# Two attention and two spectral layers on one core: unit sums rounded a round's end later, a quad's first loads spread out, output weights split earlier

## The chip, the core and the metric

The kernel runs on one core of a Trainium2 chip. The time is device microseconds (us) of one execution, and lower is better. The core's engines work side by side and wait for one another by semaphores: TensorE (PE; its weight loads are shown apart as PEld), VectorE (DVE), ScalarE (ACT), GpSimd (POOL) and SyncE (SP), which here only issues DMAs. Each engine runs its own instructions in the order in which the program emits them, so moving a line of the program moves an instruction in one or more of these queues.

## The reference, cut to what matters

```python
def _A_ref(x, wqkv, wo):                 # B, S, D = 1, 2048, 576; H, Dh, W = 32, 18, 256
    q, k, v = split_heads(x @ wqkv)
    scores = einsum("bhqd,bhkd->bhqk", q, k) * (Dh ** -0.5)
    mask = (idx[:, None] - idx[None, :] >= 0) & (idx[:, None] - idx[None, :] < W)
    p = softmax(where(mask, scores, -1e9))
    return merge_heads(einsum("bhqk,bhkd->bhqd", p, v)) @ wo

def _B_ref(x, w_r, w_i):
    return irfft2(rfft2(x) * (w_r + 1j * w_i))

x = x + _A_ref(_layernorm(x), A_wqkv, A_wo)
x = x + _B_ref(_layernorm(x), B_w_r, B_w_i)
x = x + _A_ref(_layernorm(x), A_wqkv, A_wo)
x = x + _B_ref(_layernorm(x), B_w_r, B_w_i)
```

All in float32. The kernel keeps that precision on PE by writing an operand as a rounded part (the "high" part, type fp32r in the profile) plus the remainder.

## The kernel before

Each attention layer (the change is in both, which are called layer 1 and layer 2 here) takes the 32 heads as eight **quads** n of four heads, and each quad as 16 blocks of 128 tokens. That gives 128 **value blocks** t in a row. A block of queries needs the keys of its own block and of the two before it. For every block and head there are two scores: S, by which the maximum of a row is found (`score_max`: PE L1187, then DVE L1189), ten blocks ahead (`LEAD`), and E, the score with the maximum already subtracted (`exps`: PE L1219), of which ACT takes the exponential (L1220). POOL then cuts the exponentials to the window by two selects (L1222, L1225), and PE multiplies them by the values (`part`, U, L1240); DVE turns the result (L1246).

`mixed()` runs the first 118 blocks in 59 **rounds** p = 0 to 58 of two blocks each (t = 2p and 2p + 1); the other ten blocks are the **tail**. A round has sixteen items, eight of `score_max` and eight of `exps`, and between them PE works on the projection of the queries and keys that later quads need (matmuls L1115 into `pj` and `pk`). After the items come U of the two blocks before and its turning. S, E, `pj` and `pk` live in banks of PSUM, of which E has three and S three.

The projection is cut into **units**, 128 rows of queries or keys by 512 tokens. 23 of them close within the rounds, at p = 1, 3, 5, 7, 9, 11, 13, 15, 18, 20 and so on to 48 (`ends`, two rounds apart at first, two or three from 13 on). When a unit closes in round e, ACT copies its two halves from PSUM to a staging tile `sg` (L1129; two buffers, used in turn). Four steps follow:

- `total`: POOL adds the halves, at the end of round e, as its last items.
- `high`: ACT rounds the sum (L1136).
- `remainder`: POOL subtracts the rounded part from the sum (L1142).
- `send`: SP stores both parts to `qk_d` in DRAM (L1145, 512 KB).

Where the steps stand is written out by hand with three lists for each round: `early` runs after the round's first item, `mid` after the eighth (the middle, between the exponentials of the two blocks), and `end` after the sixteenth, before U. After the eighth item, and after U, the round also calls `behind(t)`, which issues the output projection's preparations.

`loads(t)` brings queries and keys of a quad back from `qk_d` (`stack_load`, L1162), 512 tokens at a time in four **pieces** of three DMAs of 72 KB: pieces 0 and 1 are queries (`qs`), 2 and 3 keys (`ks`). Each of `qs` and `ks` has two buffers, one for the even quads and one for the odd ones. Quad 1 comes in by t = 4 to 15, one piece a block. Quad 2's first 512 tokens come at t = 12 to 15, beside quad 1's last 512 tokens. From there on each quad has one piece a block. SP issues DMAs in order, and each has to wait its turn behind the DMAs ahead of it on that queue.

The attended result goes through DRAM (`op_d`, `o_d`) to the output projection (`Out`). Its tiles (`room`) take the place of the projection's input; its weights come in five DMAs (`weights`, L744), each a fifth. `split(k)` rounds a fifth on ACT (L751) and takes the remainder (L752): on POOL for k = 0 to 2, on DVE for k = 3 and 4. `OB` is 120. The weights are loaded at t = 104 to 112 and split at t = 110 to 118, so the last split stands at the start of the tail. After the tail the attended result is read back (`oraw`) and multiplied by the weights (`ops`, L802).

Of the kernel before, what the change touches and what calls it, by code (L numbers as in the profile page):

```python
# [8 lines left out]
F32 = mybir.dt.float32  # L9
# [706 lines left out]
class Out:  # L716
# [32 lines left out]
    def split(self, k):  # L749
        c = slice(2 * self.n * k, 2 * self.n * (k + 1))  # L750
        self.nc.scalar.copy(self.w["h"][:, c], self.raw[:, c])  # L751
        (self.nc.vector if k > 2 else self.nc.gpsimd).tensor_sub(self.w["l"][:, c], self.raw[:, c], self.w["h"][:, c].bitcast(F32))  # L752

    def const(self, k):

# [110 lines left out]
def layer_a(tc, ident, eps, bp, big, src, dst, wqk_d, wv_d, wo_d, dc_d, gc_d, dram, copy, wvs, second, spectral, share):  # L866
# [17 lines left out]
    if True:  # L884
# [191 lines left out]
        with ExitStack() as c2:  # L1076
# [224 lines left out]
            def loads(t):  # L1301
                if t + LEAD in (0, 2):
                    stack_load(0, 2 + (t + LEAD) // 2)
                if t == -4:
                    stack_load(1, 0)
                n, c = divmod(t + (12 if t < 16 else 20), NT)
                if 4 <= t < 16 or 1 < n < NQ and t >= 12:
                    stack_load(1 if t < 16 else n, t // 4 if t < 16 else c // 4, (t % 4,))
                if 12 <= t < 16:
                    stack_load(2, 0, (t % 4,))  # L1310
                if t + LEAD == 5:
                    v_load(0)
                if t + 12 in range(NT, NX, NT):
                    v_load((t + 12) // NT)
# [24 lines left out]
            def mixed():  # L1339
# [4 lines left out]
                early, mid, end = {}, {}, {}  # L1344
                plan = lambda d, p, f, *a: d.setdefault(p, []).append((f, a))
# [5 lines left out]
                for p in range(last):  # L1351
# [33 lines left out]
                    done += n  # L1385
                    for total, high, remainder, send in ended:
                        total()
                        for f in (high, remainder):
                            plan(mid, p + 1, f)
                        plan(mid, p + 2, send)  # L1390
                    ended.clear()
                    run(end, p)
                    if p:
# [6 lines left out]
                    else:  # L1400
                        if p:
                            n, c = divmod((2 * p - 1) // 4, 4)
# [15 lines left out]
            OB = NX - 8  # L1418
            out = Out(nc, eps, bp, big, o_d, srcv, dstv, wo_d, dc_d, gc_d, second)

            def behind(t):
                if copy and t >= 32 and t % 4 == 0 and t < 32 + 16 * len(copy):

                    z, r = divmod(t // 4 - 8, 4)
                    P.dma_start(*[a[32 * r:32 * r + 32] for a in copy[z]])
                if t == OB - 16:
                    out.room()
                if t - OB + 16 in range(0, 10, 2):
                    out.weights((t - OB + 16) // 2)
                if 0 <= t - (OB - 10) < 10 and t % 2 == 0:  # L1430
                    out.split((t - (OB - 10)) // 2)
                if t - OB + 13 in range(0, 10, 2):
                    out.const((t - OB + 13) // 2)
                if t == OB - 3:
                    out.filters()
                if t - OB + 8 in range(0, 10, 2):
                    out.load_x(((t - OB + 8) // 2 + 1) % 5)
                if 0 <= t - (OB - 8) < 6:
                    out.attended(*divmod(t - (OB - 8), 2))
                if t - OB in (1, 2):  # L1440
                    out.attended(3, t - OB - 1)
                if t == OB + 4:
                    out.ahead_of_last()
                if t - OB - 5 in (0, 1, 2):
                    out.turn(t - OB - 5, V)
                if t == NX:

                    A.activation(wp.tile([128, 1], F32, name="se", bufs=1), eps, AF.Sqrt)
# [90 lines left out]
```

## Time and profile before

| | before |
|---|---|
| time, median of 3 runs | 1326.73 us (1315.5, 1326.73, 1673.2) |
| the profiled execution's own time | 1323.85 us |
| its span in the trace | 1322.1 us |
| mean granted clock of PE in it | 0.994 |
| rounds of layer 1, layer 2 (in the trace, from 128.8 and 805.7 us) | 59 each, mostly 4.9 to 5.5 us |

The profile gives the busy time of each engine, the waits (which instruction's idle time was ended by which other one), groups of instructions by line, and stretches of time with each engine's busy time. In a row of the time-ordered view the first number is the start, the second the duration in us, then the engine, the line and the tiles (out<-in); "x4" folds four instructions, and a bracket says how long the engine had stood idle before and what ended that. A row of the stretches has start:end, then length, and for PE, PEld, DVE, ACT and POOL the busy time with the number of instructions; the last three numbers are the granted clock (1.00 is full speed), the DMA engines' mean busy share, and GB/s.

### The profile page before, as it was taken

What the parts mean: (1) busy time and instruction counts of PE and PEld (TensorE: products, weight loads), DVE (VectorE), ACT (ScalarE), POOL (GpSimd) and SP (SyncE); (2) the same over time, 40 slices, a digit from 0 to 9 for tenths busy, and PEclk for the clock granted to TensorE, in tenths of its full rate; (3) what the DMA queues carried; (4) which work ended last, traced back from release to release, by engine and by line L of the source; (5) the groups of instructions that cost most, each with busy time, mean ns of one, the idle gap of its engine ahead of it and who ended that gap; (6) DMA issues with size and microseconds to landing.
All of it is one profiled execution on the core that took longest, in us unless ns stands there. A gap on an engine that the chain in (4) does not pass through costs nothing.

```text
span 1322.1 us, 35482 instructions
## 1 busy us (share of the span) xinstructions
PE 1281.5 (97%) x12115; PEld 1005.3 (76%) x12115; DVE 956.0 (72%) x3196; ACT 777.0 (59%) x1944; POOL 771.0 (58%) x1248
## 2 busy tenths in 40 slices
PE   8999999999999899999999999999999999899998
PEld 8986666666678699975999976666666686897687
DVE  5417889889899577757674148888889896676755
ACT  5522777878777545533355315777877778473233
POOL 2258777898776443567221196788878767113811
PEclk9999999999999999999999999999999999999999
DMA  6846666665566646688873368576665667498874
GB/s 202 220 153 206 209 199 219 213 213 193 192 199 218 199 120 225 198 261 258 275 264 74 89 204 224 194 212 195 199 199 184 201 207 247 137 346 266 287 237 164
DMA packets 179497, 274.37 MB, mean 208 GB/s; under 512 B 67743, under 2 KB 77727, under 8 KB 177989
## 3 DMA queue, kind: packets, MB, share of 16 engines
q1 hardware_dynamic: 167007, 243.63, 58.7%
q0 software_dynamic: 4656, 13.44, 3.8%
q10 hardware_dynamic: 7654, 15.03, 3.2%
q8 instruction: 97, 1.59, 0.5%
q14 instruction: 83, 0.68, 0.2%
HBM read 164.54 MB, written 114.81 MB: 211 GB/s over the span
## 4 chain that ended last, share of the span: by engine, by line
PE 80%; ACT 6%; DMA 5%; DVE 4%; issue 2%; SPq 1%; POOL 1%; DVEq 0%; ACTq 0%; POOLq 0%
PE U L1240 11%; PE pj L1115 10%; PE vps L1005 9%; PE S L1187 8%; PE ops L802 7%; PE pk L1115 6%; PE E L1219 6%; PE po L274 4%; ACT P L1220 4%; PE pq L524 3%; PE p L503 2%; PE pf L274 2%; PE pi L600 2%; PE pz L312 1%; DMA ks<-qk_d 1%
## 5 line engine op out<-in xcount | busy, mean ns | idle before, releaser
L1189 DVE CUSTOM_DVE_ANT_0 jk<-S,mask 128x384 bf16<-128x384 f32 (+2 forms) x1024 | 482.8, 527 | 35.1 <-PE S L1187 13.3
L1220 ACT ACTIVATE P<-E 128x384 f32<-128x384 f32 (+2 forms) x1024 | 409.3, 487 | 95.4 <-PE E L1219 49.7
L1219 PE MATMUL E<-qs,ks 64*128 64x384 f32 (+2 forms) x1024 | 324.3, 372 | 7.2 <-ACT P L1220 4.5
L1187 PE MATMUL S<-ks,qs 63*128 63x384 f32 (+2 forms) x1024 | 325.0, 370 | 5.6 <-DMA qs<-qk_d 2.7
L1222 POOL TENSOR_SCALAR_AFFINE_SELECT P<-P 128x512 f32<-128x512 f32 x256 | 162.3, 634 | 133.5 <-ACT P L1220 125.3
L1219 PEld LDWEIGHTS E<-qs,ks 64*128 64x128 f32 x1024 | 180.6, 185 | 63.1 <-ACT P L1220 42.1
L1187 PEld LDWEIGHTS S<-ks,qs 63*128 63x128 f32 x1024 | 172.7, 185 | 66.0 <-DVE m L1189 37.8
L1240 PE MATMUL U<-P,vq 128*32 128x256 f32 (+2 forms) x3840 | 185.1, 329 | 0.0
L1240 PEld LDWEIGHTS U<-P,vq 128*32 128x32 f32 (+1 forms) x3840 | 107.1, 109 | 75.4 <-POOL P L1225 16.3
L1115 PE MATMUL pj<-xh,wqh 64*128 64x512 f32 (+1 forms) x360 | 154.9, 430 | 0.0
L1225 POOL TENSOR_SCALAR_AFFINE_SELECT P<-P 128x512 f32<-128x512 f32 x224 | 144.0, 643 | 0.0
L1115 PE MATMUL pj<-xh,wql 64*128 64x512 f32 (+1 forms) x360 | 138.6, 425 | 0.0
L1115 PE MATMUL pj<-xl,wqh 64*128 64x512 f32 (+1 forms) x288 | 120.4, 418 | 0.0
L802 PE MATMUL ops<-oroom 128*128 128x290 f32 (+1 forms) x812 | 114.0, 297 | 1.7 <-DVE ofree L848 1.2
L802 PEld LDWEIGHTS ops<-oroom 128*128 128x128 f32 x812 | 110.4, 189 | 2.3 <-ACT ofree L836 1.5
L1115 PE MATMUL pk<-xh,wqh 64*128 64x512 f32 x230 | 92.2, 401 | 0.0
L1115 PE MATMUL pk<-xh,wql 64*128 64x512 f32 x230 | 91.1, 400 | 0.0
L1246 DVE STREAM_TRANSPOSE us<-U 128x256 f32<-128x256 f32 x128 | 57.1, 446 | 46.6 <-PE U L1240 45.6
L1189 DVE DVE_READ_ACCUMULATOR2_ANT m<- 128x1 f32 x1024 | 84.9, 83 | 0.0
L1115 PE MATMUL pk<-xl,wqh 64*128 64x512 f32 x184 | 73.1, 397 | 0.0
L1115 PEld LDWEIGHTS pj<-xh,wqh 64*128 64x128 f32 (+1 forms) x360 | 66.8, 186 | 7.5 <-issue 1.5
L789 POOL TENSOR_TENSOR oroom<-oraw,oroom 64x128 fp32r<-64x128 f32 x26 | 13.9, 535 | 99.1 <-ACT oroom L787 49.2
(522 smaller groups left out, 2869.6 us busy)
## 6 DMA issues: line engine op xcount, KB each, us to landing
qk_d<-sg SPq DMA_DIRECT2D x56, 512.0 KB
qs<-qk_d SPq DMA_DIRECT2D x384, 72.0 KB
ks<-qk_d SPq DMA_DIRECT2D x348, 72.0 KB
op_d<-o SPq DMA_DIRECT2D x56, 256.0 KB
v_d<-vt SPq DMA_DIRECT2D x32, 304.0 KB
vq<-v_d SPq DMA_DIRECT2D x16, 608.0 KB
wt<-in_w SPq DMA_DIRECT2D x16, 580.0 KB
ofree<-x SPq DMA_DIRECT2D x16, 580.0 KB
```

The costliest lines, as they stand in the source:

```text
L274: T.matmul(ps[:, c, 0:NF], tail[r] if si == 4 else hl_(si), dcs[b // 2][r, b % 2], start=mi == si == 0, stop=si == 4)
L802: self.nc.tensor.matmul(self.ps[u][n][:, 0:self.n], x, self.w[p][:, (2 * wk + n) * self.n:(2 * wk + n + 1) * self.n], start=first and i == ...
L1005: T.matmul(ps[:, n, 0:288], xT(xk, c), w[:, wk, n * 288:(n + 1) * 288], start=i == 0, stop=i == len(ks) - 1)
L1115: T.matmul(ps.rearrange("r (n p) -> r n p", n=NT) if second else ps, w[r, wk], x[r], start=s == 0, stop=s == len(ks) - 1)
L1187: T.matmul(ps[:, 0:N], q[b:b + 63, pair, i * 128:i * 128 + 128], k[b:b + 63, pair, lo:hi], start=True, stop=True)
L1189: V.tensor_tensor_reduce(out=jk[:, 0:N], in0=ps[:, 0:N], in1=mask[:, 384 - N:384], scale=1.0, scalar=-3e38, op0=ALU.add, op1=ALU.max, accu ...
L1219: T.matmul(ps[:, 0:nq], k[b:b + 64, pair, j * 128:j * 128 + 128], q[b:b + 64, pair, j * 128:j * 128 + nq], start=True, stop=True)
L1220: A.activation(p[:, hl_, 0:nq], ps[:, 0:nq], AF.Exp, scale=SC)
L1222: P.affine_select(out=p[:, :, 0:128], in_=p[:, :, 0:128], pattern=[[0, 4], [1, 128]], compare_op=ALU.is_ge, fill=0.0, base=0, channel_mult ...
L1225: P.affine_select(out=p[:, :, 256:384], in_=p[:, :, 256:384], pattern=[[0, 4], [-1, 128]], compare_op=ALU.is_gt, fill=0.0, base=0, channel ...
L1240: T.matmul(U[32 * h:32 * h + v.shape[1], (q0 - e) * 128:(q1 - e) * 128], v, pt[n, j][:, h, (q0 - j) * 128:(q1 - j) * 128], start=j == max( ...
L1246: V.transpose(us[n, c][:, 8 * k:8 * k + 8].rearrange("r b (a p) -> r (b a) p", a=2), U[:, 0:256].rearrange("r (p n) -> r n p", n=NT))
```

## The change

Four places change. The rounding `high` goes from the middle of round e + 1 to its end, `remainder` from there to the early list of round e + 2, and `send` from the middle of round e + 2 to its end. Quad 2's first four pieces are loaded at t = 6, 8, 10 and 12 instead of 12 to 15. The output's `room` and weights come at t = 98 to 106 instead of 104 to 112 and are split at t = 104 to 112 instead of 110 to 118 (the rounds in the title of the change count value blocks t). The remainders of all five fifths are taken by POOL.

```diff
--- before.py
+++ after.py
@@ -749,7 +749,7 @@
     def split(self, k):
         c = slice(2 * self.n * k, 2 * self.n * (k + 1))
         self.nc.scalar.copy(self.w["h"][:, c], self.raw[:, c])
-        (self.nc.vector if k > 2 else self.nc.gpsimd).tensor_sub(self.w["l"][:, c], self.raw[:, c], self.w["h"][:, c].bitcast(F32))
+        self.nc.gpsimd.tensor_sub(self.w["l"][:, c], self.raw[:, c], self.w["h"][:, c].bitcast(F32))
 
     def const(self, k):
 
@@ -1306,8 +1306,8 @@
                 n, c = divmod(t + (12 if t < 16 else 20), NT)
                 if 4 <= t < 16 or 1 < n < NQ and t >= 12:
                     stack_load(1 if t < 16 else n, t // 4 if t < 16 else c // 4, (t % 4,))
-                if 12 <= t < 16:
-                    stack_load(2, 0, (t % 4,))
+                if t in range(6, 14, 2):
+                    stack_load(2, 0, ((t - 6) // 2,))
                 if t + LEAD == 5:
                     v_load(0)
                 if t + 12 in range(NT, NX, NT):
@@ -1385,9 +1385,9 @@
                     done += n
                     for total, high, remainder, send in ended:
                         total()
-                        for f in (high, remainder):
-                            plan(mid, p + 1, f)
-                        plan(mid, p + 2, send)
+                        plan(end, p + 1, high)
+                        plan(early, p + 2, remainder)
+                        plan(end, p + 2, send)
                     ended.clear()
                     run(end, p)
                     if p:
@@ -1423,12 +1423,12 @@
 
                     z, r = divmod(t // 4 - 8, 4)
                     P.dma_start(*[a[32 * r:32 * r + 32] for a in copy[z]])
-                if t == OB - 16:
+                if t == OB - 22:
                     out.room()
+                if t - OB + 22 in range(0, 10, 2):
+                    out.weights((t - OB + 22) // 2)
                 if t - OB + 16 in range(0, 10, 2):
-                    out.weights((t - OB + 16) // 2)
-                if 0 <= t - (OB - 10) < 10 and t % 2 == 0:
-                    out.split((t - (OB - 10)) // 2)
+                    out.split((t - OB + 16) // 2)
                 if t - OB + 13 in range(0, 10, 2):
                     out.const((t - OB + 13) // 2)
                 if t == OB - 3:
```

On ACT, layer 1, round 6 (the unit `sg_3` closed in round 5; `P_12` and `P_13` are the exponentials of the round's two blocks). Before:

```order
L1220 ACTIVATE P_12_3124<-E_0_3125 128x384
L1220 ACTIVATE P_12_3124<-E_1_3136 128x384
L1220 ACTIVATE P_12_3124<-E_2_3139 128x384
L1220 ACTIVATE P_12_3124<-E_3_3148 128x384
L1136 CAST sg_3_3081<-sg_3_3081 128x512
L1220 ACTIVATE P_13_3170<-E_0_3171 128x384
L1220 ACTIVATE P_13_3170<-E_1_3180 128x384
L1220 ACTIVATE P_13_3170<-E_2_3183 128x384
L1220 ACTIVATE P_13_3170<-E_3_3192 128x384
```

and with the change, the same place:

```order
L1220 ACTIVATE P_12_3124<-E_0_3125 128x384
L1220 ACTIVATE P_12_3124<-E_1_3136 128x384
L1220 ACTIVATE P_12_3124<-E_2_3139 128x384
L1220 ACTIVATE P_12_3124<-E_3_3148 128x384
L1220 ACTIVATE P_13_3168<-E_0_3169 128x384
L1220 ACTIVATE P_13_3168<-E_1_3178 128x384
L1220 ACTIVATE P_13_3168<-E_2_3181 128x384
L1220 ACTIVATE P_13_3168<-E_3_3190 128x384
L1136 CAST sg_3_3080<-sg_3_3080 128x512
```

The rounding moved from between the two blocks' exponentials to behind the last one. The same holds at 46 places, 23 in each layer.

On SP, layer 1, about rounds 5 to 7 (`qs_1058` and `ks_1060` are the buffers of quads 0 and 2, `qs_1059` and `ks_1061` those of quad 1; L1203 writes the maxima of a row beside the queries). Before:

```order
L1203 DMA qs_1059<-mt_0_2213 2x4x128 x2
L1162 DMA qs_1059<-qk_d 18x2x512 x3
L1162 DMA qs_1058<-qk_d 18x2x512 x3
L1162 DMA qs_1059<-qk_d 18x2x512 x3
L1162 DMA qs_1058<-qk_d 18x2x512 x3
L1162 DMA ks_1061<-qk_d 18x2x512 x3
L1162 DMA ks_1060<-qk_d 18x2x512 x3
L1275 DMA op_d<-o_1_2309 128x512
L1145 DMA qk_d<-sg_3_2182 128x2x512
L1162 DMA ks_1061<-qk_d 18x2x512 x3
L1162 DMA ks_1060<-qk_d 18x2x512 x3
L1203 DMA qs_1059<-mt_1_2445 2x4x128 x2
```

and with the change:

```order
L1203 DMA qs_1059<-mt_0_2222 2x4x128 x2
L1162 DMA qs_1059<-qk_d 18x2x512 x3
L1162 DMA ks_1060<-qk_d 18x2x512 x3
L1162 DMA qs_1059<-qk_d 18x2x512 x3
L1162 DMA ks_1061<-qk_d 18x2x512 x3
L1275 DMA op_d<-o_1_2313 128x512
L1162 DMA ks_1061<-qk_d 18x2x512 x3
L1145 DMA qk_d<-sg_3_2190 128x2x512
L1203 DMA qs_1059<-mt_1_2445 2x4x128 x2
```

Of quad 2's four pieces only the last one (`ks_1060`) still stands among quad 1's last four, and the send of `sg_3` stands behind quad 1's last piece instead of ahead of it. The other three pieces have moved to rounds 3, 4 and 5.

On DVE, layer 1, the last round (58). Before:

```order
L1189 ISA jk_1_0_7964,m_3_7823<-S_1_0_7962,mask 128x384
L1189 ISA m_3_7823 128x1
L752 TENSOR_TENSOR oroom<-ofree,oroom 128x576
L1189 ISA jk_0_1_7972,m_3_7823<-S_0_1_7970,mask 128x384
L1189 ISA m_3_7823 128x1
```

and with the change:

```order
L1189 ISA jk_1_0_7968,m_3_7829<-S_1_0_7966,mask 128x384
L1189 ISA m_3_7829 128x1
L1189 ISA jk_0_1_7974,m_3_7829<-S_0_1_7972,mask 128x384
L1189 ISA m_3_7829 128x1
L1189 ISA jk_1_1_7984,m_3_7829<-S_1_1_7982,mask 128x384
```

The subtraction of the output weights no longer stands between the maxima; it is on POOL, six blocks sooner.

## The prediction

> **What bounds the kernel now.** I read the page's shares first, then who waits for whom, then the value rounds one by one. TensorE (PE) looks like the bound:
>
> ```profile
> PE 1281.5 (97%) x12115; PEld 1005.3 (76%) x12115; DVE 956.0 (72%) x3196; ACT 777.0 (59%) x1944; POOL 771.0 (58%) x1248
> ```
>
> But a busy PE is modelled, and the waits name a partner:
>
> ```profile
> PEld E L1219 <- ACT P L1220: 42.1, 137, 1.3
> POOL P L1222 <- ACT P L1220: 125.3, 155, 3.8
> ```
>
> 137 times PE's weight load for the second score (E) stands until ACT has emptied a bank by an exponential; GpSimd (POOL) mostly waits for ACT too, so it keeps up. The rounds say when. Here are six pairs of rounds from layer 1, by their stretches (start:end, length, then busy time of PE, PEld, DVE, ACT, POOL). The two of a pair have the same place in a quad (p mod 8): p = 24 and 40, 26 and 42, 13 and 29, 22 and 38, 39 and 23, 41 and 25. In the second of each, the rounding of a unit (high, L1136) stands between the exponentials.
>
> ```profile
> 255.38:260.29 4.91, 4.91 (x65) 3.39 (x64) 4.81 (x18) 4.52 (x11) 3.21 (x7) 1.00 0.60 185
> 336.68:341.84 5.16, 5.16 (x63) 3.37 (x62) 4.95 (x18) 3.98 (x10) 4.76 (x7) 1.00 0.38 119
> 265.01:269.92 4.91, 4.91 (x63) 3.41 (x62) 4.81 (x18) 4.53 (x11) 4.31 (x8) 1.00 0.58 165
> 346.32:351.71 5.39, 5.32 (x64) 3.50 (x63) 5.10 (x19) 4.32 (x12) 5.39 (x8) 1.00 0.42 121
> 199.13:204.26 5.13, 5.13 (x68) 3.39 (x65) 4.50 (x19) 4.35 (x10) 3.48 (x7) 1.00 0.78 250
> 280.55:286.04 5.49, 5.39 (x67) 3.36 (x63) 4.58 (x19) 3.82 (x9) 5.48 (x8) 1.00 0.78 229
> 245.17:250.09 4.92, 4.92 (x63) 3.42 (x62) 4.82 (x18) 4.54 (x11) 4.40 (x9) 1.00 0.55 180
> 326.46:331.61 5.15, 5.15 (x65) 3.40 (x64) 4.94 (x18) 3.95 (x10) 5.14 (x8) 1.00 0.36 107
> 331.61:336.68 5.07, 5.07 (x67) 3.59 (x64) 4.49 (x19) 3.23 (x10) 3.34 (x6) 1.00 0.79 275
> 250.09:255.38 5.29, 5.19 (x69) 3.72 (x65) 4.68 (x20) 2.97 (x10) 5.06 (x7) 1.00 0.87 264
> 341.84:346.32 4.48, 4.48 (x51) 2.91 (x47) 4.34 (x19) 3.82 (x10) 2.31 (x5) 1.00 0.75 247
> 260.29:265.01 4.72, 4.72 (x52) 2.88 (x49) 4.64 (x20) 3.81 (x10) 4.18 (x6) 1.00 0.76 250
> ```
>
> PE issues the same work in both of a pair and shows as full in both, yet the second takes 0.25, 0.48, 0.36, 0.23, 0.22 and 0.24 us longer: 0.30 on the mean. So PE is not what sets a round; a loop of PE, DVE and ACT is, and a cast of ACT in its middle stretches it. What comes next is DVE: it is busy 4.81 of 4.91 in the short rounds, so they can't go much lower than these pairs show.
>
> **The cast, moved.** Round 12 shows how, in time order:
>
> ```profile
> 196.00 0.64 ACT L1136 CAST sg<-sg 128x512 fp32r<-128x512 f32 x1
> 196.51 1.67 ACT L1220 ACTIVATE P<-E 128x384 f32<-128x384 f32 x4
> 197.08 0.18 PEld L1219 LDWEIGHTS E<-qs,ks 64*128 64x128 f32 x1 [0.34 <-ACT P L1220]
> ...
> 199.64 1.66 ACT L1220 ACTIVATE P<-E 128x384 f32<-128x384 f32 x4 [1.46 <-PE E L1219]
> ...
> 203.05 0.61 ACT L1129 COPY sg<-pj 128x512 f32<-128x512 f32 x1
> ```
>
> The cast holds up the second block's exponentials, E waits 0.34 us for its bank, and the last score and U behind it on PE start late. After its last exponential ACT then idles 1.46 us while PE does U. There the change puts the 0.64 us cast, so it is hidden; if that cover were gone, it would cost the next round's first exponential 0.64 us at most. In round 13 (199.13 to 204.26, the short one of its pair) the copies of a closing unit stand at that very place (203.05), and cost nothing there. The cast waits for GpSimd's sum, made one round before; behind it wait the exponentials of the next round. The price per rounding is between 0 (all of it given back) and 0.48 (the largest pair); I take the mean, 0.30. There are 23 a layer; those of p = 2 and 8 stand beside a wait for a DMA, so I count 21: 42 × 0.30 = **12.6 us**.
>
> The remainder goes from the middle of round e+1 to the start of e+2 on GpSimd: 1.28 us (L1142, below) leave the round where POOL was busy 4.76 of 5.16 and enter one with 3.21 of 4.91. Behind it wait the selects of that round, which PE reads only in the next round's U: a round of cover, so nothing. The send follows it on SyncE (SP), half a round later; the loads that read it come at least four rounds after the unit closes. Nothing, unless SP jams (last rival).
>
> **The loads, spread.** SP runs ahead of the rounds until a wait stops it. Round 8 ends in a stall in both layers:
>
> ```profile
> 142.86 1.05 SPq L1162 DMA_DIRECT2D ks<-qk_d  x3
> 147.46 0.36 SPq L896 DMA_DIRECT2D wqr<-in_wqk  x1
> ...
> 161.44 4.46 SPq L1162 DMA_DIRECT2D qs<-qk_d  x12
> 165.94 2.95 SPq L1162 DMA_DIRECT2D ks<-qk_d  x6
> ...
> 169.45 1.58 SPq L1145 DMA_DIRECT2D qk_d<-sg  x1
> 171.08 3.00 SPq L1162 DMA_DIRECT2D ks<-qk_d  x6
> ...
> 176.95 0.41 PE L1187 MATMUL S<-ks,qs 63*128 63x384 f32 x1 [1.59 <-DMA qs<-qk_d]
> ...
> 853.28 0.41 PE L1187 MATMUL S<-ks,qs 63*128 63x384 f32 x1 [1.21 <-DMA ks<-qk_d]
> ```
>
> The first S of round 9 needs the last piece of quad 1, issued from 171.08 on, 5.9 us before PE gets it. Ahead of it from 161.44 on stand 18 DMAs, three pieces of quad 1 and three of quad 2 (three DMAs each), and the send of 1.58 us. Now one of them goes into SP's idle stretch from 143.91 to 147.46, two into rounds 4 and 5 (ahead of pieces of quad 1 that round 7 needs; the first of those sits behind a shorter wait, since the send there steps back too), only one stays between quad 1's last pieces, and the send stands behind. That is two pieces fewer after 161 (about 1.05 us each, by the first row) and 1.58: up to 3.7 us sooner, of which the two moved to rounds 4 and 5 may give 2.1 back as a later start. Between 1.6 and 3.7, against a stall of 1.59 and 1.21 and a round 9 that starts about 0.9 us earlier through the casts: I take the stalls as gone, **2.8 us**; at worst they stay.
>
> The first stall also costs clock. These are stretches on the grid of 3.41 us on which the granted clock changes (the third number from the end), then rounds 9 of the two layers:
>
> ```profile
> 175.47:178.88 3.41, 1.68 (x12) 1.32 (x14) 1.55 (x6) 0.82 (x3) 0.55 (x1) 1.00 0.46 138
> 178.88:182.29 3.41, 3.41 (x20) 3.00 (x18) 2.63 (x9) 2.40 (x7) 1.22 (x2) 0.50 0.78 267
> 448.51:451.92 3.41, 1.68 (x34) 0.76 (x32) 2.35 (x5) 1.93 (x4) 0.85 (x2) 1.00 0.91 217
> ...
> 176.95:183.38 6.43, 6.17 (x47) 4.80 (x47) 4.67 (x18) 4.30 (x10) 1.94 (x4) 0.73 0.68 225
> 853.28:858.11 4.83, 4.76 (x49) 3.30 (x49) 4.15 (x18) 3.86 (x10) 1.59 (x3) 1.00 0.54 176
> ```
>
> After a stretch with PE busy 1.68 of 3.41 us the clock was halved for one stretch, and round 9 took 6.43 instead of 4.83: **1.6 us**, which go with the stall. The stretch at 448.51, just as idle, was spared: it stands on the edge. With everything before it shifted on the grid it will more likely be caught, so I set **1.6 us against** it. The Trainium skill ("TensorE: Matmul & The Clock Gate", section "HAM oscillation") has as its abstract rule "no PE-idle gaps >~3.4µs". By that a stall of 1.59 us would halve nothing, and none of the 1.6 would follow from it; the trace agrees with the page on the grid of 3413 ns, not on the length of the gap.
>
> **The output weights.** Per layer five ACT casts and five subtractions; two of these go from DVE to GpSimd.
>
> ```profile
> L752 POOL TENSOR_TENSOR oroom<-ofree,oroom x6: 1407/1414/1428, 414.5 to 1100.8; 128x576 fp32r<-128x576 f32 x3, 128x580 fp32r<-128x580 f32 x3
> ...
> L1142 POOL TENSOR_TENSOR sg<-sg x46: 1266/1282/1297, 142.5 to 1060.8; 128x512 fp32r<-128x512 f32 x46
> ...
> 428.98 0.69 ACT L751 CAST oroom<-ofree 128x576 fp32r<-128x576 f32 x1
> 429.70 0.79 DVE L752 TENSOR_TENSOR oroom<-ofree,oroom 128x576 fp32r<-128x576 f32 x1 [0.32 <-ACT oroom L751]
> ...
> 435.44 0.67 ACT L751 CAST oroom<-ofree 128x576 fp32r<-128x576 f32 x1
> 436.00 12.29 ACT L1220 ACTIVATE P<-E 128x384 f32<-128x384 f32 x34
> ```
>
> Rounds 52, 53 and 54 each get a cast in their middle: +3 × 0.30, by the pairs. Round 57 loses its one: −0.30. In round 58 DVE no longer waits 0.32 and subtracts 0.79 between scores: −1.1. In the tail ACT is without a pause for 12.29 us, so the cast at 435.44 counts in full: −0.56. Sum −1.1 a layer, **2.1 us**; at worst nothing, if the chain of DMAs behind (oraw) keeps its time. The two extra subtractions of 1.41 us lie on GpSimd in rounds that hold no remainder any more. On that queue the selects stand behind them, with a round of cover. The five weight loads on SP (L744) come up to three rounds sooner, just after the last unit has closed (round 48) and its buffers are free; they now stand ahead of the last pieces of quad 7, whose first reader is ten blocks away: nothing.
>
> **Sum.** 12.6 + 2.8 + 1.6 − 1.6 + 2.1 = 17.5 us against the profiled run (1323.85, 2.9 below the median of 1326.73): **1306.4**, said as 1306.5.
>
> **Rivals.** (a) PE is the bound, as 97% says, or the cast only moves its delay to the next round's start: the 12.6 are lost, 1319. The pairs speak against it. (b) SP is as late as before, since three pieces still precede: stalls and half clock stay, 1306.5 + 4.4 = 1311. (c) The halved stretch comes whatever the stall, as by the page's rule: 1308. (d) Slower: two staging buffers hold the units. A send that comes half a round later must land before the copies of the unit after next, about two rounds on. ACT has waited so once:
>
> ```profile
> 139.58 1.64 ACT L1220 ACTIVATE P<-E 128x384 f32<-128x384 f32 x4 [1.26 <-DMA qk_d<-sg]
> ```
>
> If a send lands over 10 us after the start of round e+2, every unit but the first two pays that: 42 × 1.26 = 53, so 1359. Against it: subtraction 1.28, SP's issue 1.58 and the 5.9 us of the late load add up to 8.8.
>
> **Chances.** Forecast 0.64, (a) 0.13, (b) 0.14, (c) 0.05, (d) 0.04. The low end takes 0.48 a rounding (−7.6): 1299, less one halved stretch: 1297. The high end takes in (a) and one stretch: 1321. Two undisturbed runs differ by 11 us, so about 2% is what can be told from no change. Under 1300.2, 2% below the median, I see 0.13 (the lower end of the forecast's own range); slower by 2% only by most of (d), 0.03.
>
> **What would show it.** Right: rounds 40 and 42 at 4.9, E's waits for ACT down from 42 to about 28 us (42 x 0.34 less), no S that waits for a DMA at round 9, ACT's 34 exponentials in the tail starting with no weight cast before them. Wrong: rounds of 5.15 as before, an ACT copy L1129 that waits for a DMA, or POOL that gates U.

## The result, and the profile after

| | before | with the change |
|---|---|---|
| median | 1324.39 us (11 runs) | 1308.37 us (11 runs, 1305.69 to 1313.46) |
| ratio | | 0.9891, 95% interval 0.9873 to 0.9909 |
| profiled execution, span | 1323.85, 1322.1 us | 1308.3, 1306.6 us |

The change makes the kernel 1.1% faster, 16.0 us by the medians and 15.5 by the spans of the two profiles. One of the eleven runs before, of 1673.2 us, stands far above the others (1315.5 to 1327.43) and is not in the ratio; without it the medians differ by 15.6 us. The forecast was 1306.5, by a sum of 17.5.

The shares of the whole span, then the row of the waits for E, both of the kernel after:

```profile
PE 1271.4 (97%) x12115; PEld 1004.0 (77%) x12115; DVE 950.9 (73%) x3192; ACT 784.7 (60%) x1944; POOL 777.0 (59%) x1252
...
PEld E L1219 <- ACT P L1220: 28.3, 105, 2.5
```

PE's share is 97% as before and tells nothing. E waits for ACT 28.3 us instead of 42.1. Where the difference shows in time is seen round by round. These are the stretches of rounds 38, 40, 42, 29, 25 and 23 of layer 1 after (start:end, length, busy time of PE, PEld, DVE, ACT, POOL, granted clock, DMA share, GB/s); each is the second of one of the forecast's pairs:

```profile
320.26:325.17 4.91, 4.91 (x63) 3.40 (x62) 4.81 (x18) 4.14 (x10) 4.90 (x9) 1.00 0.57 159
330.25:335.16 4.91, 4.91 (x63) 3.38 (x62) 4.82 (x18) 4.16 (x10) 3.85 (x7) 1.00 0.60 198
339.64:344.71 5.07, 5.07 (x64) 3.62 (x64) 4.92 (x19) 4.53 (x12) 4.72 (x8) 1.00 0.46 131
275.23:280.36 5.13, 5.13 (x67) 3.38 (x63) 4.49 (x19) 3.91 (x9) 5.12 (x8) 1.00 0.80 238
255.62:260.11 4.49, 4.49 (x52) 2.91 (x49) 4.44 (x20) 3.93 (x10) 3.27 (x5) 1.00 0.76 267
245.41:250.70 5.29, 5.18 (x68) 3.72 (x64) 4.67 (x20) 3.07 (x10) 4.05 (x7) 1.00 0.89 277
```

They took 5.15, 5.16, 5.39, 5.49, 4.72 and 5.29 us before: the first five fall by 0.24, 0.25, 0.32, 0.36 and 0.23, and round 23 by nothing. Over the 42 rounds that I counted the fall is 10.0 us. The rounds e + 2, into which POOL's subtraction of 1.28 us moved, do not pay for it: 42 of the 46 keep their length to 0.02 us, one grows by 0.28 and one falls by 0.20 (rounds 5 and 13 of layer 2), and the two round 9 change for other reasons, told below. ACT in round 12, in time order, shows the cast in its new place:

```profile
191.29 1.64 ACT L1220 ACTIVATE P<-E 128x384 f32<-128x384 f32 x4
193.11 1.72 ACT L1220 ACTIVATE P<-E 128x384 f32<-128x384 f32 x4 [0.18 <-PE pk L1115]
194.70 0.63 ACT L1136 CAST sg<-sg 128x512 fp32r<-128x512 f32 x1
196.22 0.49 ACT L1220 ACTIVATE P<-E 128x384 f32<-128x384 f32 x1 [0.89 <-PE E L1219]
```

The second four exponentials follow the first with a pause of 0.18, and behind the cast ACT still idles 0.89.

The other places: rounds 8 and 9 of layer 1, then of layer 2, and the first S of layer 2's round 9; then round 2 of layer 1 with what ACT and PE wait for in it.

```profile
170.88:175.79 4.91, 4.91 (x63) 3.41 (x62) 4.81 (x18) 4.18 (x10) 3.36 (x6) 1.00 0.67 213
175.79:180.27 4.48, 4.48 (x51) 2.89 (x47) 4.44 (x20) 3.81 (x10) 3.27 (x5) 1.00 0.76 252
837.38:842.72 5.34, 5.01 (x63) 3.42 (x63) 5.18 (x19) 4.17 (x10) 3.77 (x7) 1.00 0.62 214
842.72:847.18 4.46, 4.46 (x47) 3.11 (x47) 4.19 (x19) 3.83 (x10) 2.85 (x5) 1.00 0.55 169
842.72 0.41 PE L1187 MATMUL S<-ks,qs 63*128 63x384 f32 x1 [0.34 <-DMA ks<-qk_d]
...
136.62:145.43 8.81, 6.73 (x63) 5.17 (x63) 4.70 (x17) 4.71 (x12) 4.34 (x7) 0.81 0.87 302
139.65 0.87 ACT L1220 ACTIVATE P<-E 128x384 f32<-128x384 f32 x2 [2.39 <-DMA qk_d<-sg]
140.20 0.64 PE L1219 MATMUL E<-qs,ks 64*128 64x384 f32 x1 [2.08 <-ACT P L1220]
```

The stall at round 9 is gone in layer 1, with the halved clock, and down from 1.21 to 0.34 in layer 2; rounds 8 and 9 together lose 3.9 and 1.5 us. But round 2 of layer 1 grew from 6.54 to 8.81: the send that ACT waits for there lands at about 139.6 in both profiles, this time the rounds began 1.3 us earlier, so PE stood idle for 2.08 us and the clock was halved behind it. The change moves nothing ahead of that point, and it is not the change that did this: in the eleven kernels whose opening is that of before, round 2 of layer 1 takes anything from 6.05 to 9.05 us, 9.02 with the output weights alone moved, which are no part of a layer's first rounds.

At the end of a layer: rounds 52, 53, 54 and 57 of layer 1 and round 53 of layer 2 after; then three rows of before, round 52 of layer 1 and round 53 of the two layers; then E's waits in layer 2's round 53 and in both tails.

```profile
388.90:394.14 5.24, 5.15 (x77) 4.24 (x76) 5.00 (x18) 4.00 (x10) 3.69 (x6) 1.00 0.61 210
394.14:399.59 5.45, 5.36 (x81) 4.37 (x77) 4.58 (x19) 3.74 (x9) 4.49 (x7) 1.00 0.86 242
399.59:404.83 5.24, 5.15 (x77) 4.22 (x76) 5.00 (x18) 4.00 (x10) 4.71 (x8) 1.00 0.67 216
415.39:419.85 4.46, 4.46 (x67) 3.83 (x63) 4.32 (x18) 3.37 (x8) 2.46 (x5) 1.00 0.94 297
1061.53:1067.73 6.20, 5.61 (x81) 4.30 (x78) 4.82 (x19) 3.74 (x9) 4.50 (x7) 1.00 0.81 226
```

```profile
396.67:401.57 4.90, 4.90 (x78) 4.16 (x78) 4.80 (x18) 3.64 (x9) 2.80 (x6) 1.00 0.60 188
401.57:406.67 5.10, 5.10 (x82) 4.30 (x79) 4.61 (x20) 3.38 (x8) 3.15 (x6) 1.00 0.78 230
1076.71:1081.82 5.11, 5.11 (x83) 4.31 (x79) 4.62 (x20) 3.37 (x8) 3.15 (x6) 1.00 0.83 253
```

```profile
1062.34 0.41 PE L1219 MATMUL E<-qs,ks 64*128 64x384 f32 x1 [0.38 <-DMA qs<-mt]
432.39 0.44 PE L1219 MATMUL E<-qs,ks 64*128 64x384 f32 x2 [1.06 <-DMA qs<-mt]
1100.02 0.44 PE L1219 MATMUL E<-qs,ks 64*128 64x384 f32 x2 [0.80 <-DMA qs<-mt]
```

A weight cast in the middle costs its round 0.35, against 0.24 on the mean for a unit's cast. Layer 2's round 53 pays 0.75 more, with a new wait of 0.38: E for the rows of the maxima (`qs<-mt`), which SP now issues behind the weight loads. The two waits in the tails are new too, but there the last weight load was issued 30 us before the rows that E waits for (395.74 and 426.26 in layer 1), so its place on SP's queue does not explain them.

### The profile page after: what moved, and what is told of

It is laid out like the page before. It is cut to its first block, busy times and chain, and to the rows that moved or that the text cites. A ratio compares the mean times of both kernels' runs of the same rounds, so it can differ in the third digit from the quotient of the medians.

```text
span 1306.6 us, 35490 instructions
## 1 busy us (share of the span) xinstructions
PE 1271.4 (97%) x12115; PEld 1004.0 (77%) x12115; DVE 950.9 (73%) x3192; ACT 784.7 (60%) x1944; POOL 777.0 (59%) x1252
## 3 DMA queue, kind: packets, MB, share of 16 engines
q8 instruction: 97, 1.59, 0.5%
## 4 chain that ended last, share of the span: by engine, by line
PE 79%; DMA 8%; ACT 4%; DVE 4%; POOL 2%; issue 2%; SPq 1%; DVEq 0%; ACTq 0%; POOLq 0%
PE pj L1115 11%; PE U L1240 11%; PE vps L1005 9%; PE S L1187 8%; PE pk L1115 7%; PE ops L802 7%; PE E L1219 5%; PE po L274 4%; PE pq L524 3%; PE p L503 2%; PE pf L274 2%; ACT P L1220 2%; PE pi L600 2%; DMA op_d<-o 2%; PE pz L312 2%
## 5 line engine op out<-in xcount | busy, mean ns | idle before, releaser
L1219 PE MATMUL E<-qs,ks 64*128 64x384 f32 (+2 forms) x1024 | 320.8, 369 | 8.2 <-ACT P L1220 4.2
L1219 PEld LDWEIGHTS E<-qs,ks 64*128 64x128 f32 x1024 | 179.9, 185 | 55.4 <-ACT P L1220 28.3
L1115 PE MATMUL pj<-xh,wqh 64*128 64x512 f32 (+1 forms) x360 | 151.9, 422 | 0.0
```

The source lines that it names most:

```text
L1115: T.matmul(ps.rearrange("r (n p) -> r n p", n=NT) if second else ps, w[r, wk], x[r], start=s == 0, stop=s == len(ks) - 1)
L1219: T.matmul(ps[:, 0:nq], k[b:b + 64, pair, j * 128:j * 128 + 128], q[b:b + 64, pair, j * 128:j * 128 + nq], start=True, stop=True)
```

## The experiments

Each round below is compared with the same round of the other profile; a change of one round without a wait for a DMA is sure to about 0.02 us there, one of the whole time only to some 3 us. Rounds in which something waits for a DMA (2, 9, 25 and 53 above all) differ by 1 to 3 us between profiles, also where nothing ahead of them was changed.

**The rounding alone.** Only the three `plan` lines of the change, on the kernel before.

> The kernel before with only the unit sum's three steps moved (rounding at the end of round e+1, remainder early and send at the end of round e+2). Theory A (a cast in the middle of a round holds up the exponentials): the rounds e+1 fall by as much as in the changed kernel, about 0.24 us each, 10 us over both layers; the stall at the start of round 9 shrinks from 1.59 and 1.21 us only by the send that now stands behind the loads; time about 1313 us against 1324. Rival B (the gain of those rounds came from the loads or from POOL's lighter middle): rounds 40 and 42 stay at 5.15 and 5.39, time within 3 us of before.

1314.91 us against 1322.88; ratio 0.9927, interval 0.9901 to 0.9954. Rounds 40 and 42 of it, then round 9 of both layers and what E waits for in them:

```profile
334.51:339.43 4.92, 4.92 (x63) 3.40 (x62) 4.82 (x18) 4.18 (x10) 3.86 (x7) 1.00 0.60 191
343.90:348.98 5.08, 5.08 (x65) 3.63 (x64) 4.93 (x19) 4.54 (x12) 4.75 (x8) 1.00 0.47 133
...
178.30:184.50 6.20, 4.73 (x51) 3.28 (x47) 4.59 (x19) 3.82 (x10) 3.21 (x5) 1.00 0.58 193
847.12:853.46 6.34, 4.78 (x52) 3.31 (x49) 4.61 (x20) 3.86 (x10) 3.24 (x5) 1.00 0.59 183
180.20 0.41 PE L1219 MATMUL E<-qs,ks 64*128 64x384 f32 x1 [1.47 <-DMA qs<-mt]
849.12 0.41 PE L1219 MATMUL E<-qs,ks 64*128 64x384 f32 x1 [1.56 <-DMA qs<-mt]
```

The casts give the whole 10.0 us (5.09 and 4.96 by layer) without the other edits. The stall of S at round 9 turns into one of E, 1.47 and 1.56 us: with all the loads still ahead, and the send now right ahead of the rows of the maxima on SP's queue, these come late. That I had not expected.

**The loads alone.** Only the two `stack_load` lines of the change.

> The kernel before with only quad 2's first loads spread over t = 6 to 12. Theory A: two pieces fewer (about 1 us of issue each) stand ahead of quad 1's last piece, so PE's wait for a DMA at round 9 falls from 1.59 and 1.21 us to nothing, and with it the halved clock of layer 1's round 9; rounds 8 and 9 together lose 4.5 us in layer 1 and 1.2 us in layer 2; no round of the other ones changes; time about 1319 to 1321. Rival B (the send ahead of the loads is what makes them late): the wait stays over 1 us and the time at 1324.

1322.21 against 1322.88; ratio 0.9983, interval 0.9965 to 1.0001. Round 6 of the two layers, and the first S behind the second:

```profile
161.46:167.20 5.74, 5.22 (x64) 3.41 (x64) 5.37 (x19) 3.95 (x10) 5.62 (x8) 1.00 0.70 231
838.73:844.73 6.00, 5.22 (x63) 3.41 (x63) 5.38 (x19) 3.95 (x10) 5.75 (x8) 1.00 0.60 207
844.73 0.41 PE L1187 MATMUL S<-ks,qs 63*128 63x384 f32 x1 [0.78 <-DMA ks<-qk_d]
```

Rounds 8 and 9 lose 2.9 us in layer 1, of it 2.0 in round 9, whose clock was not halved (on this see the run with the send in its place, below), and 1.6 in layer 2. Round 6 gives 0.59 and 0.85 back: the pieces put into rounds 4 and 5 delay those that round 7 needs, and its first S waits (in layer 1 for 0.52 us, which the view puts down to DVE). The forecast named this as a possible loan. In the changed kernel it isn't due: its round 6 takes 4.91 and 4.94. It comes back in other kernels with both edits, though: 5.67 in layer 2 with two casts at the end, 5.87 in layer 1 with the three moves below. So each edit alone trades one late DMA for another, and only the two together clear round 9 of layer 1 (with the loads alone its first S still waits 0.62 us, put down to DVE).

**The output weights alone.** The last hunk and the `tensor_sub` line of the change.

> The kernel before with only the output weights loaded and split six blocks sooner, all remainders on POOL. Theory A: rounds 52, 53 and 54 each grow by 0.35 us (a cast in their middle), round 57 falls by 0.35, round 58 to the output's first matmul falls by about 1.0: net -0.3 us a layer, time 1323 to 1325, no difference to be seen. Rival B: POOL's two extra subtractions of 1.41 us or the five loads ahead on SP's queue cost more than they give, rounds 52 to 57 grow by 2 us or more a layer, time 1327 or more. Rival C (the forecast's size): -1.1 us a layer, 1322.

1323.53 against 1322.88; ratio 0.9999, interval 0.9976 to 1.0022. Rounds 52, 53, 54 and 57 change by +0.35, +0.84, +0.36 and -0.35 in layer 1 and by +0.36, +0.63, +0.35 and -0.36 in layer 2; from round 58 to the output's first matmul it is 1.51 and 0.94 us less. Theory A, to its number, but for round 53, which adds 0.49 and 0.28. Here is layer 1's, and the first E in it:

```profile
402.89:408.82 5.93, 5.60 (x81) 4.29 (x77) 4.80 (x19) 3.73 (x9) 4.47 (x7) 1.00 0.82 219
403.41 0.18 PEld L1219 LDWEIGHTS E<-qs,ks 64*128 64x128 f32 x1 [0.34 <-issue]
```

The view names no DMA for the 0.34 us, but the rows of the maxima that this E reads land at 403.30. The last kernel below tells whether it is the weight loads.

**The cast with its remainder, the send as it was.** On the kernel before; the remainder stands right behind the cast, on POOL:

```diff
-                        for f in (high, remainder):
-                            plan(mid, p + 1, f)
+                        plan(end, p + 1, high)
+                        plan(end, p + 1, remainder)
                         plan(mid, p + 2, send)
```

> The kernel before with the rounding (and the remainder right behind it on POOL) at the end of round e+1, and the send in the middle of round e+2 as it was. Theory A (only the cast's place on ACT matters): rounds e+1 fall by the same 0.24 us on the mean, 10 us in all, and the wait of S at round 9 stays near 1.59 and 1.21 us, since the send stands ahead of the loads again; about 1313 to 1316. Rival B (the remainder has to leave the round for it): rounds e+1 fall by less than 0.1, or the next round's selects come late and U waits for POOL; 1320 or more.

1313.04 against 1324.39; ratio 0.9907, interval 0.9875 to 0.9939. Rounds 40 and 42 fall to 4.91 and 5.06 as in the changed kernel, the 21 rounds of layer 2 by 4.87 together (those of layer 1 by 3.73, since round 23 grew by 1.31 here). The send, back in its place, keeps the stall:

```profile
333.88:338.79 4.91, 4.91 (x63) 3.39 (x63) 4.82 (x18) 4.17 (x10) 3.87 (x7) 1.00 0.57 177
177.71 0.41 PE L1187 MATMUL S<-ks,qs 63*128 63x384 f32 x1 [1.99 <-DMA qs<-qk_d]
177.71:182.28 4.57, 4.57 (x48) 3.27 (x48) 4.08 (x17) 3.83 (x10) 1.58 (x3) 1.00 0.57 183
```

The first row is round 40, the last round 9. So it is ACT's order that counts in the rounds, and the send's place on SP that counts at round 9. Round 9 also shows that the stall and the halved clock are not one thing: here S stands for 1.99 us, longer than the 1.59 of before, and the round runs at full clock and takes 4.57 and not 6.43. It is the same in layer 1 with the output weights alone (1.39 us, then 4.44), while in that run's layer 2 a stall of 0.76 and one of 1.08 brought a halved stretch and a round of 7.25.

**The cast twice, in the middle and at the end.** `high` issues its copy a second time, once in the kernel before and once in the changed one:

```diff
                         def high():
                             A.copy(sg[:, 0], raw[:, 1])
+                            if half is not None:
+                                A.copy(sg[:, 0], raw[:, 1])
```

> The kernel before with each unit's rounding on ACT done twice in the middle of round e+1 (the second one writes the same values): 46 more casts of 0.64 us there. Theory A: what a cast costs in the middle isn't its length but what is left after the loop's slack (0.24 of 0.64 us for the first), so the second has no slack left and costs nearly all of its 0.64: 38 to 42 times, 24 to 27 us, about 1348. Lower end, if the slack repeats: 0.24 each, 1333. Rival B (ACT is off the path, PE is the bound): no change, 1323.

> The changed kernel with each unit's rounding done twice at the end of round e+1, behind the last exponential. Theory A (hidden there: ACT idles about 1.4 us while PE does U): 46 more casts cost nothing, rounds as in the changed kernel within 0.05, about 1308. Rival B (the delay moves to the next round's first exponential): 0.3 to 0.64 each, 12 to 27 us, 1320 to 1335.

In the middle: 1347.8 against 1324.39, ratio 1.0164 (1.0135 to 1.0193). At the end: 1309.18, ratio 0.9870 (0.9843 to 0.9896). Round 40 and the wait for E with two casts in the middle, then round 40 with two at the end (lines below the copy count two higher in these kernels):

```profile
346.21:352.03 5.82, 5.19 (x64) 3.37 (x63) 5.00 (x18) 4.58 (x11) 5.24 (x8) 1.00 0.38 110
PEld E L1221 <- ACT P L1222: 72.2, 138, 2.1
```

```profile
326.89:331.80 4.91, 4.91 (x64) 3.39 (x64) 4.81 (x18) 4.49 (x11) 3.87 (x7) 1.00 0.64 205
```

Without a cast in its middle the round takes 4.92 us, with one 5.16, with two 5.82. The first costs 0.24 of its 0.64 us, since a round has about 0.4 us of slack there, and the second costs 0.64 to 0.66 in 36 of the 42 rounds: there is no slack left. At the end two cost nothing in the same rounds (0.00 to 0.03, but for one round 6 with a wait for a DMA); the rounds behind two of them, 26 and 50, grow by 0.12 to 0.15 in both layers, so the cover is just used up there. That settles the main step, and the price by which it is to be worked out: length less slack.

**The send a round later.** The forecast's slower case, made to happen: `plan(end, p + 3, send)` in the changed kernel.

> The changed kernel with the send one more round later (end of round e+3). It is the forecast's slower case made to happen: two staging buffers, whose next use is the copies of the unit after next. In the changed kernel a send lands 2.8 to 7 us (two rounds between units) or 9 to 11 us (three) ahead of these copies. One round later takes about 5 us of it: some ten copies a layer would wait 0.3 to 2.6 us for a DMA. Theory A: those waits show on ACT's copies (L1129) and cost 10 to 25 us in all, 1318 to 1333. Rival B: ACT's idle time at the end of a round covers them, and the time stays at 1308 to 1311.

1321.15 us, ratio to before 0.9970 (0.9948 to 0.9992): 13 us of the change's 16 are gone, by the medians. The profiled run is the fastest of the nine (1316.22) and shows 8 of them. ACT's copies wait for the sends, eleven times in both layers where ten a layer were foreseen:

```profile
ACT sg L1129 <- DMA qk_d<-sg: 13.4, 11, 2.6
```

Of these 13.4 us 9.5 show in the 42 rounds e+1; ACT's idle time at the end of a round takes a part. The mechanism is real and was some 2 to 3 us of margin away; its size is 8 to 13 us and not the 53 that I set for it.

**The splits at the ends of rounds.** In the changed kernel, one block later:

```diff
-                if t - OB + 16 in range(0, 10, 2):
-                    out.split((t - OB + 16) // 2)
+                if t - OB + 15 in range(0, 10, 2):
+                    out.split((t - OB + 15) // 2)
```

> The changed kernel with the five splits of the output weights one block later, that is behind U at the end of rounds 52 to 56 and not in their middle. Theory A (place of a cast on ACT): rounds 52 to 56 lose 0.35 us each, 3.5 us over both layers, time about 1305 against 1308.4. Rival B (it is POOL's subtraction of 1.41 us in these rounds that costs, or the loads): no round falls by more than 0.1, time 1308, or more if the subtraction now stands ahead of the next round's selects and U waits for them.

1306.39 us; ratio to before 0.9862 (0.9837 to 0.9886). Rounds 53 and 54 of layer 1:

```profile
392.70:397.86 5.16, 5.16 (x81) 4.27 (x77) 4.69 (x20) 3.31 (x8) 4.59 (x7) 1.00 0.74 187
397.86:402.95 5.09, 4.96 (x78) 4.09 (x77) 4.88 (x18) 4.53 (x11) 4.81 (x8) 1.00 0.78 256
```

Rounds 52 and 53 lose 0.35 and 0.29, but 54 and 56 only 0.16 and 55 nothing; 1.0 us in layer 1 and 1.3 in layer 2 (where 0.64 of it is round 53, with less of the wait for the rows). From the start of round 58 to the end of the tail's last E it is another 0.29 and 0.65. Round 54 takes 4.89 in the kernel before, with no split near; what keeps it at 5.09 here isn't known.

**One more cast moved, by the same reasoning.** The projection's own weights are rounded by ACT (L698) 0.9 us into rounds 3, 11, 20, 28 and 37; here at the end of the next round:

```diff
-                        w_split(i + 1)
+                        (w_split(i + 1) if half is None else splits.append(i + 1))
...
                     ended.clear()
+                    while splits:
+                        plan(end, p + 1, w_split, splits.pop(0))
```

> The changed kernel with one more cast moved on the same reasoning: the rounding of the projection's own weights (L698 on ACT, 0.72 us, with its remainder on POOL, 1.55 us) from 0.9 us into rounds 3, 11, 20, 28 and 37 to the end of the round after. Theory A (a cast among the exponentials stretches its round): these ten rounds fall from 5.45, 5.45, 5.29, 5.28 and 5.49 us to what their neighbours without it take, 0.3 to 0.4 us each, 3 to 4 us in all, and rounds 4, 12, 21, 29 and 38 stay (two casts at the end, 1.3 us, fit in ACT's idle 1.4); time about 1305 against 1308.4. Rival B (POOL's 1.55 us subtraction is what stretches them): the stretch moves to the next rounds, 1308.

Round 11 of the changed kernel, then of this one:

```profile
185.33:190.78 5.45, 5.45 (x69) 3.58 (x65) 3.41 (x20) 4.76 (x11) 5.45 (x7) 1.00 0.71 216
```

```profile
185.32:190.26 4.94, 4.94 (x67) 3.44 (x63) 3.33 (x20) 4.28 (x10) 4.01 (x6) 1.00 0.72 253
```

All ten rounds fall, by 0.34 to 0.51 us, 4.1 us together, and the rounds behind them stay. Yet the time is 1307.74, ratio 0.9880 (0.9855 to 0.9905), no different from the changed kernel's: in the profile waits for DMAs and halved clocks elsewhere took it back (layer 1's round 25 is 1.48 us longer, layer 2's round 2 by 1.79). This profile is of the slowest of the six runs (1315.67), so it shows more of that than the median has. A part is the edit's own: round 15 takes 5.29 to 5.31 us in both layers of the three kernels that have it, and 5.05 to 5.08 in all the others; rounds 6 and 9 are longer in most of these layers too, by 0.1 to 1.0. For round 25 it isn't settled: it grew by 1.08 in the profile of the output weights alone too, where nothing had changed ahead of it.

**Round 2's wait.** The opening's four sends issued by ACT:

```diff
-                            (nc.scalar if i < 2 else nc.sync).dma_start(qk_d
+                            (nc.scalar if i < 2 or i == 2 and half is None else nc.sync).dma_start(qk_d
```

> The changed kernel with the sends of the four units (2, c) of the opening issued by ACT and not by SP. It is about round 2, where ACT's first exponential waits 2.39 us (layer 1) and 1.37 us (layer 2) for a send to land that SP issued only at 134.69, behind a weight load, six loads and the 608 KB of vq. Theory A (SP's order made it late): issued by ACT at about 125, the send lands before round 2, the wait goes, round 2 falls from 8.81 and 6.31 to about 5.0, in layer 1 with the halved clock that followed it; 4 to 5 us, 1304. Rival B (the DMA engines were full, it lands as late from any queue): the wait stays over 1 us and the time at 1308; or ACT, which now waits for the remainder before it issues, delays the opening by 1 us or more.

1307.17 us; ratio 0.9884 (0.9861 to 0.9906). Round 2 of the two layers:

```profile
138.86:143.93 5.07, 5.07 (x63) 3.62 (x62) 4.38 (x17) 4.53 (x12) 4.16 (x7) 1.00 0.33 69
804.42:809.50 5.08, 5.08 (x63) 3.62 (x63) 4.38 (x17) 4.53 (x12) 4.16 (x7) 1.00 0.32 86
```

Theory A holds for the wait: 8.81 and 6.31 became 5.07 and 5.08. But layer 1's first round begins at 129.86 and no longer at 127.52. In the opening S now waits for a load, and the clock is halved behind it:

```profile
123.54 0.59 PE L1187 MATMUL S<-ks,qs 63*128 63x384 f32 x3 [1.53 <-DMA qs<-qk_d]
```

The same wait (1.44 and 1.94) and the same halving stand in the two kernels below, which have this edit, and not in the eleven others, where no S waits over 0.52 us there and the clock stays. So in layer 1 2.3 of the 3.7 us come back as another stall; 1.4 there and layer 2's 1.2 are what is left.

**The three together, and the weight loads back in their old place.** The last kernel differs from the one before it in the blocks at which the weights are loaded (t = 104 to 112) and split (ends of rounds 54 to 58).

> The changed kernel with the three moves together: splits of the output weights and the projection weights' rounding at the ends of rounds, and the opening's four sends from ACT. Theory A (they lie at different places and add up): 3.5 + 3.5 + about 1 to 3 us off 1308.4, so 1299 to 1301. Rival B (what leaves one place comes back as a wait for a DMA elsewhere, since every gain brings the rounds nearer to the landings): under 4 us gained, 1304 or more.

> As the kernel with the three moves, but the output weights are loaded where they were before the change (t = 104 to 112) and split at the ends of rounds 54 to 58. It is about round 53, where with the loads at t = 98 to 106 E waits for the maxima's rows (DMA qs<-mt) in most profiles, 0.1 to 1 us and once 2. Theory A (the weight loads ahead on SP's queue and the 1.45 MB they bring make those rows late): no wait for qs<-mt in rounds 52 and 53, which take 4.9 and 5.1 us; time 0.3 to 2 us under the other. Rival B: the wait comes all the same, or moves into the tail, where the last split now stands two rounds later; time equal or 1 us over the other.

1306.71, ratio 0.9865 (0.9826 to 0.9904), and 1305.7, ratio 0.9858 (0.9820 to 0.9895). Round 53 of layer 1 with the three, with its wait; then of the last:

```profile
395.45:401.74 6.29, 5.41 (x82) 4.30 (x78) 5.03 (x20) 3.31 (x8) 4.59 (x7) 1.00 0.70 201
396.77 0.41 PE L1219 MATMUL E<-qs,ks 64*128 64x384 f32 x1 [0.88 <-DMA qs<-mt]
```

```profile
394.00:399.10 5.10, 5.10 (x82) 4.29 (x78) 4.62 (x20) 3.38 (x8) 3.16 (x6) 1.00 0.82 235
```

With the loads back, rounds 52, 53 and 54 take 4.89, 5.10 and 4.89 in both layers and no E waits there, so the wait at round 53 came from the weight loads. The other profiles agree: round 53 is longer than its casts account for in 11 of the 16 layers with the early loads and in none of the 12 without. The waits for these rows in the tail go with the early loads in the same way (on PE in 11 of 16 tails, and in none of 12), though how they do is not shown.

For the whole, the medians side with rival B of the first text: three moves that each take 2 to 5 us out of their rounds give no more than the first of them alone. The best medians, 1305.7 and 1306.39, are 2 to 3 us under the changed kernel's, and their intervals overlap its own. They don't exclude theory A, whose 1301 us is a ratio of 0.9826 and so lies at the lower edge of both intervals; and in the last kernel's profile, of its second shortest run (1301.54), with three halved stretches as in the changed kernel's, rounds 2 to 57 are 9.9 us shorter than there and the span 6.8. Whether the moves add up is open.

## Why the prediction was right, step by step

The total was met; its terms were met less well, and that they add up to it is in part luck. From the two profiles (spans, so 15.5 in all):

| step | forecast | measured |
|---|---|---|
| 42 casts out of the middle | 12.6 | 10.0 |
| stalls and clock at rounds 8, 9 | 2.8 + 1.6 | 5.3 |
| another stretch halved instead | -1.6 | -2.3 |
| output weights, rounds 52 to 57 | -1.2 | -2.2 |
| output weights, round 58 to the first matmul | +3.3 | +1.8 |
| not in the sum: opening 1.3, stages behind attention 2.0, other rounds -0.4 | 0 | 2.9 |
| sum | 17.5 | 15.5 |

Three of the measured terms are differences between two runs rather than the work of the change: 2.0 of the 5.3 (the halved clock of layer 1's round 9), the -2.3 (round 2) and the 2.9. What is left is 10.0 + 3.3 - 2.2 + 1.8, about 13 us, which lies within the 12 to 17 us of the interval for the whole time.

- **The casts.** The mechanism is shown by the experiments (the rounding alone, the cast with the send as it was, doubled in the middle, doubled at the end), the size was off: 0.24 a cast and not 0.30. The step that failed is the mean over six pairs. POOL's subtraction moved with the cast each time, so the two were never parted; that the cast makes the 0.24 is borne out by the doubled casts, which add nothing on POOL, and by the rounds e + 2, which take the subtraction at no cost. In the pair of rounds 39 and 23 the cast cost nothing, and of the 0.48 between 42 and 26 it made 0.32; the rest was other work, since round 42 takes 5.07 and round 23 still 5.29 with no cast in their middle. Rounds 23 and 31 hold the narrow exponentials of a quad's last two blocks, and ACT was busy only 2.97 of 5.29 us in round 23: that row was quoted and should have told that a cast is free there. Of the forecast's marks, E's waits of about 28 us came out at 28.3, round 40 at 4.91 and round 42 at 5.07 instead of 4.9; no weight cast stands among the tail's exponentials. Of its marks of being wrong none showed: no copy L1129 waits for a DMA in the changed kernel.
- **The stalls at round 9.** Right in place and size, though "gone" was true in layer 1 only. What I had not seen is that it takes both edits: the send and the loads each bring a wait of their own. "1.6 us, which go with the stall" was a matter of luck: two kernels that keep the stall in layer 1 (1.39 and 1.99 us) run round 9 at full clock, so how the stall lies on the grid counts, and the profile of before was one in which it was caught.
- **The halved stretch.** I set it to the layer's tail; between the two profiles it fell on round 2, and that is luck too: the change moves nothing ahead of it, and round 2 of layer 1 has a halved stretch in seven of the eleven kernels with the opening of before. The profile of before was one of the four without. The forecast had named that round as one with a wait for a DMA, and left out that a wait whose end is fixed by a DMA grows when the rounds ahead begin sooner, as they do by chance here.
- **The output weights.** "The five weight loads on SP: nothing" failed: they make the rows of the maxima late, 0.75 us in round 53 of layer 2. The tail gave 0.96 and 0.85 of the 1.66 a layer; the new waits of 1.06 and 0.80 for such rows stand there, which the loads' place on SP's queue does not explain. Measured alone, the edit gives nothing (0.9999).
- **The unclaimed 2.9 us** are no work of the change that the experiments show. The opening ends between 126.8 and 130.5 us in the nine other kernels whose opening is that of before; the stages between the two layers' attention had a halved stretch (at 574.8) before and none after, and behind layer 2's attention both profiles have two.
- **The rivals.** PE as the bound is refuted by the doubled casts: 0.65 us more of ACT's work lengthened rounds in which PE shows as busy throughout in the kernel before. The staging buffers' case exists, some 2 to 3 us away. Its price of 1.26 us was misread: the row is an exponential's wait in round 2, not a copy's. The opening's sums are staged in buffers of the exponentials' own tiles (`P`), and ACT waits there until such a buffer has been sent. The copies' own waits, in the run with the later send, were 0.2 to 2.6 us, eleven times.

## What to carry to other kernels

An engine with a low share can still set a round by where in its order an instruction stands: ask what stands behind it and who waits for that, and price the move as its length less the slack, not by its length. Doubling the suspect in both places is a cheap and sharp test of this. In a kernel that many DMA waits punctuate, gains of 2 to 5 us in the rounds need not show in the median: an earlier start can turn into a longer wait for a landing that has not moved, so look at which landing becomes the new end before counting on the sum. And before a difference of two profiles is put down to a change, look for the same place in other profiles in which nothing ahead of it differs: of the 15.5 us here, some 7 us up and down were such differences.

## What the runs showed of the hardware

The clock is not halved by a gap of one length. In the fourteen profiles, on the grid of 3.41 us and up to the last stretch of the program, 54 stretches at full clock were followed by a halved one: every stretch in which PE stood idle over 1.80 us (42 of them), 12 of the 47 with 1.33 to 1.80 us, and none below. The idle time may be one stall or several. The Trainium skill ("TensorE: Matmul & The Clock Gate", section "HAM oscillation") names gaps over some 3.4 us; the traces agree on the grid and not on the length. The number of halved stretches, two to eight in a profile at about 1.7 us each (an estimate: half of 3.41), is large enough for most of the 2 to 17 us by which runs of one kernel differ. The record has the granted clock of each run, and over its 151 runs the two go together: against the mean of its own kernel, a run is 1.1 us longer for each us that its clock says was lost (one less the granted clock, times the span), with a correlation of 0.81. So the clock goes with some 65% of the variance between runs; what makes up the rest isn't shown.
